# Sixteen float32 attention items with the softmax divided after the product

## The chip, the core and the metric

The kernel runs on one core of a Trainium2 chip. The metric is the device time of the whole program in microseconds (us). PE is TensorE (matrix products), PEld its weight loads, DVE is VectorE, ACT is ScalarE, POOL is GpSimd, SP issues the DMAs.

## What is computed

Windowed attention with a linear position bias, and two MLPs behind it, all in float32:

```python
B, H, S, D = 4, 8, 576, 64;  window = 128
scores = q @ k.T / sqrt(D)                       # per batch b and head h
scores = where(0 <= i - j < window, scores - slope[h] * (i - j), -1e9)
attn = exp(scores - max(scores, -1))
attn = attn / (sum(attn, -1) + 1e-9)
x = (attn @ v), heads side by side               # 2304 tokens x 512
h1 = x @ w_in;   x2 = (max(h1, 0) + alpha * min(h1, 0)) @ w_out     # d_ff = 2048
h2 = x2 @ w_in2; out = (h2 * sigmoid(1.702 * h2)) @ w_out2
```

## The kernel before

The attention is cut into 64 items (batch, part, head). Part 0 is the first 256 queries of a batch, in two chunks of 128: the first sees 128 keys, the second 256. Items 0 to 15 (part 0 of batches 0 and 1, `FP = 2 * H`) are computed with plain float32 products; from item 16 on operands are split into a high and a low half. Only items 0 to 15 are touched by the change. For such an item n the steps are:

- `a_qk` (L342): scores s in PSUM, two products with a 64-row operand.
- `a_bias` (L362, DVE): adds the bias, writes the negated scores to tt in SBUF and their row minimum to st.
- `a_exp` (L378, ACT): exponential of each chunk with the row extreme taken off, and the row sums into st.
- `a_recip` (L386, L387) and `a_norm` (L398), DVE: reciprocal of the sums, and each chunk times its reciprocal.
- `a_trans` (L411): three transposes of 128 x 128 through TensorE into pt in PSUM; `a_pt_hi` (L418, ACT) copies them to SBUF.
- `a_av` (L432): product with v as the stationary operand and pt as the moving one, one of 256 columns and one of 128; a float32 product is two passes, so four matrix records. vz is v of one head in its half of 128 columns, with zeros in the other half, so that an even and an odd head add up in one bank x.
- `a_x3` (L479 ACT, L107 DVE): x of a pair of heads is split into xh and xl, the input of the first MLP, feature-major.

Beside this, weights are decoded: they come as pairs of words through SP's DMA queue into four buffers ws; ACT scales (L147, L150), DVE shifts and adds (L154, L159), ACT casts the high half wh (L102) and DVE subtracts for the low half wl (L107). Layer 1 has 32 such chunks, two for each of 16 hidden slices.

The first loop (items 0 to 9) is the prologue; the second runs the MLP of a block of 256 tokens, one step f for a hidden slice: `m1_h` (L493) makes h from xh and xl, ACT and DVE make g and its halves gh and gl (L508, L518, L522, L107), and `m1_o` (L544) adds the product with the second weights, two steps later. Every second step carries one more attention item. Block 0 needs the x of items 0 to 7, that is four pairs; in block 0 the weight chunks are still being decoded. "gl 13" is the low half of g in step f = 13 of block 0.

The program is written in that order, but a scheduler sets the order within each engine; weight decoding is kept in program order among itself. Engines work in order. PSUM has eight banks: two for h, two for the output sums (pool ps_o, tags o0 and o1), four shared by the attention (pool ps_a).

## Time and profile before

| | |
|---|---|
| median of 3 runs | 948.61 us (948.21 to 950.05) |
| the profiled execution | 951.22 us, of it span 949.4 us |
| busy in the span | PE 98%, PEld 91%, DVE 72%, ACT 55%, POOL 9% |
| chain that ended last | PE 91%, DVE 2%, issue 1% |
| granted TensorE clock, mean | 0.999 |

How to read it: busy time counts an engine from the start to the end of each instruction, so instructions that overlap or wait inside (matrix products above all) look longer than they are. Where an engine is the limit, the time from one start to the next (the pitch) says what an instruction costs. The chain follows the last instruction back through whatever released it; what lies off it can still hold a buffer or a queue.

### The profile page before, as it was taken

Reading aid. Unit: us, or ns where it says so; the run is one execution under the profiler, and the core shown is the slowest. Engines: PE = TensorE matmul, PEld = TensorE weight load, DVE = VectorE, ACT = ScalarE, POOL = GpSimd, SP = SyncE. Lnnn points to the kernel's source line nnn. Section 1 sums busy time; section 2 is a strip of 40 time slices with the busy share of each in tenths; the row PEclk is TensorE's granted clock in tenths of the full one; section 3 lists DMA queues with packets and bytes.
Section 4 is the critical chain, followed back from the end, with each engine's and each line's share of the span. In section 5 each row is a group of like instructions: output and inputs, shape, how many; then the busy total and the mean of one; then the engine's idle time right before and its main releaser. Section 6 shows DMA issues by size and latency. Waiting matters only on the chain.

```text
span 949.4 us, 17872 instructions
## 1 busy us (share of the span) xinstructions
PE 926.7 (98%) x6536; PEld 862.2 (91%) x6536; DVE 687.6 (72%) x1743; ACT 526.7 (55%) x1325; POOL 89.7 (9%) x127
## 2 busy tenths in 40 slices
PE   6899999999999999999999999999999999999997
PEld 3698899999999999999988888888898899999997
DVE  6898876778888888888457753685333798878876
ACT  5999866667667676676344443564232553433333
POOL 1100211122222222222000000000000000000000
PEclk9999999999999999999999999999999999999999
DMA  9666511223222222221023344665332333433323
GB/s 242 205 217 209 183 54 55 66 68 91 69 67 91 67 68 91 67 90 44 1 89 110 112 128 169 203 227 199 117 124 99 134 134 117 151 133 132 132 72 112
DMA packets 44041, 112.45 MB, mean 118 GB/s; under 512 B 5041, under 2 KB 15153, under 8 KB 43953
## 3 DMA queue, kind: packets, MB, share of 16 engines
q1 hardware_dynamic: 43952, 111.31, 36.1%
q8 instruction: 51, 0.84, 0.4%
q14 instruction: 38, 0.30, 0.1%
HBM read 82.98 MB, written 28.31 MB: 117 GB/s over the span
## 4 chain that ended last, share of the span: by engine, by line
PE 91%; DVE 2%; issue 1%; ACT 0%; DVEq 0%; ACTq 0%
PE h L493 21%; PE h L591 21%; PE p L658 18%; PE o L544 17%; PE p L544 5%; PE x L444 3%; PE pt L411 3%; PE s L351 1%; PE s L352 1%; PE s L342 1%; DVE wl L107 0%; DVE wd L159 0%; ACT oh L102 0%; PE x L432 0%; DVE wd L154 0%
## 5 line engine op out<-in xcount | busy, mean ns | idle before, releaser
L493 PE MATMUL h<-xh,wh 128*128 128x256 f32 (+1 forms) x512 | 151.9, 298 | 1.4 <-ACT xh L479 1.4
L493 PE MATMUL h<-xh,wl 128*128 128x256 f32 (+1 forms) x512 | 152.3, 298 | 0.0
L493 PE MATMUL h<-xl,wh 128*128 128x256 f32 (+1 forms) x512 | 151.4, 296 | 0.0
L658 PE MATMUL p<-wh,oh 128*128 128x256 f32 x504 | 136.3, 284 | 1.0 <-ACT oh L102 0.6
L658 PE MATMUL p<-wl,oh 128*128 128x256 f32 x504 | 136.2, 283 | 0.0
L544 PE MATMUL o<-gh,wl 128*128 128x256 f32 x448 | 127.5, 286 | 0.0
L544 PE MATMUL o<-gh,wh 128*128 128x256 f32 x448 | 125.9, 286 | 0.7 <-ACT gh L522 0.7
L544 PE MATMUL o<-gl,wh 128*128 128x256 f32 x448 | 125.5, 281 | 1.1 <-DVE gl L107 1.1
L658 PE MATMUL p<-wh,ol 128*128 128x256 f32 x504 | 119.2, 283 | 0.4 <-DVE ol L107 0.4
L591 PE MATMUL h<-x2h,wh 128*128 128x512 f32 (+1 forms) x320 | 117.9, 368 | 0.0
L591 PE MATMUL h<-x2l,wh 128*128 128x512 f32 (+1 forms) x320 | 117.8, 368 | 0.0
L591 PE MATMUL h<-x2h,wl 128*128 128x512 f32 (+1 forms) x320 | 117.7, 368 | 0.0
L605 DVE TENSOR_TENSOR g<-h,sg 128x512 f32<-128x512 f32 (+1 forms) x80 | 51.0, 638 | 90.7 <-ACT sg L601 90.5
L601 ACT ACTIVATE sg<-h 128x512 f32<-128x512 f32 (+1 forms) x80 | 44.4, 555 | 108.5 <-PE h L591 108.3
L493 PEld LDWEIGHTS h<-xh,wh 128*128 128x128 f32 x512 | 96.3, 189 | 5.2 <-ACT xh L479 1.9
L493 PEld LDWEIGHTS h<-xh,wl 128*128 128x128 f32 x512 | 96.6, 189 | 3.9 <-DVE wl L107 0.6
L493 PEld LDWEIGHTS h<-xl,wh 128*128 128x128 f32 x512 | 97.0, 189 | 3.0 <-issue 0.3
L658 PEld LDWEIGHTS p<-wh,oh 128*128 128x128 f32 x504 | 96.5, 192 | 2.1 <-ACT oh L102 2.0
L658 PEld LDWEIGHTS p<-wl,oh 128*128 128x128 f32 x504 | 96.7, 192 | 0.1
L518 DVE SCALAR_TENSOR_TENSOR g<-n,beta,h 128x256 f32<-128x256 f32 x112 | 53.2, 475 | 54.1 <-ACT n L508 53.8
L508 ACT ACTIVATE n<-h 128x256 f32<-128x256 f32 x112 | 42.8, 383 | 87.8 <-PE h L493 87.3
L658 PEld LDWEIGHTS p<-wh,ol 128*128 128x128 f32 x504 | 86.5, 192 | 0.7 <-DVE ol L107 0.6
(105 smaller groups left out, 2203.0 us busy)
## 6 DMA issues: line engine op xcount, KB each, us to landing
ws<-in_w_in_dram SPq DMA_DIRECT2D x32, 512.0 KB, 3.9
ws<-in_w_out_dram SPq DMA_DIRECT2D x32, 512.0 KB, 3.7
raw<-in_u_dram SPq DMA_DIRECT2D x32, 512.0 KB, 3.5
g2d<-g SPq DMA_DIRECT2D x32, 512.0 KB, 3.1
gr<-g2d SPq DMA_DIRECT2D x32, 512.0 KB, 3.2
raw<-in_u_dram SPq DMA_DIRECT2D x16, 320.0 KB, 2.8
wd<-x2d SPq DMA_DIRECT2D x36, 128.0 KB, 2.9
out_dram<-ob SPq DMA_DIRECT2D x16, 256.0 KB, 3.4
```

The costliest lines, as they stand in the source:

```text
L342: nc.tensor.matmul(o[:, :keys], raw[:, c0 : c0 + rows], raw[:, 256 + kk : 256 + kk + keys], start=True, stop=True)
L351: nc.tensor.matmul(o[:, :n_], q, kh[:, ks : ks + n_], start=True, stop=False)
L411: nc.tensor.transpose(banks[bank][:, dst : dst + P], src, ident)
L444: nc.tensor.matmul(x[:, oc : oc + nq], v, p[:, col : col + nq], start=(i == 0 and k == 0), stop=(i == len(js) - 1 and k == 1), skip_group_ ...
L493: nc.tensor.matmul(ph, w[:, 0, c * P : (c + 1) * P], x[:, c, r : r + n], start=(c == 0 and i == 0), stop=(c == NC - 1 and i == 2),)
L508: nc.scalar.activation(n, ph, AF.Relu, scale=-1.0)
L518: nc.vector.scalar_tensor_tensor(g, n, beta[:, f : f + 1], ph, op0=ALU.mult, op1=ALU.add)
L544: nc.tensor.matmul(o, w[:, 1, c * P : (c + 1) * P], g, start=(f == 0 and (k == KM or c % 2 == 0) and i == 0), stop=(f == NF - 1 and i == 2 ...
L591: nc.tensor.matmul(ph[:, :n], w[:, f % 2, c * P : (c + 1) * P], x[:, c, :n], start=(c == 0 and i == 0), stop=(c == NC - 1 and i == 2),)
L601: nc.scalar.activation(sg[:, :n], ph[:, :n], AF.Sigmoid, scale=1.702)
L605: nc.vector.tensor_tensor(g[:, f % 2, :n], ph[:, :n], sg[:, :n], op=ALU.mult)
L658: nc.tensor.matmul(o[:, m, :], g[:, a, m * P : (m + 1) * P], w, start=(p == 0 and m == 0 and i == 0), stop=(p == NF // 2 - 1 and i == 2), ...
```

## The change

For items 0 to 15 the division moves behind the product. `f_sub` takes the row extreme off the negated scores in SBUF (first chunk on DVE, second on ACT). `a_trans` transposes these scores instead of the weights of the softmax, and `f_exp` takes the exponential while reading the transposes from PSUM and writes pt. `f_av` turns the product: pt is the stationary operand, and the moving one is v with a column of ones behind it, 65 columns, so that column 64 of the result is the sum. Per item there are three such products, into a bank xq that an even and an odd head share. `f_div` (every odd item, DVE) adds 1e-9 to the four columns of sums, takes the reciprocal and multiplies, into xq in SBUF, with queries on the partitions. `a_x3` first transposes xq back with two transposes into a bank x. `a_exp`, `a_recip`, `a_norm` and `a_pt_hi` do nothing for these items. For items below 8 the two banks are those of the output sums, idle until the first `m1_o`; for items 8 to 15 they come from the four shared ones. In the loops `f_exp` stands first in an item's turn, and `a_x3` comes one item earlier than before.

```diff
@@ -261,7 +261,8 @@
-    vzs = [apf.tile([P, 2, P], F32, name=f"vz{i}") for i in range(2)]
+    vzs = [apf.tile([P, 2, D + 1], F32, name=f"vz{i}") for i in range(2)]
+    xq = apf.tile([P, 2, 2, D], F32, name="xq")
@@ -324,8 +325,7 @@
         if n < FP:
-            d0 = (h % 2) * D
-            nc.gpsimd.tensor_copy(vzs[n % 2][:, :, d0 : d0 + D], vr)
+            nc.gpsimd.tensor_copy(vzs[n % 2][:, :, :D], vr)
             return
@@ -371,8 +371,28 @@
+    @stage
+    def f_sub(n, b, u, h, U):
+        if n >= FP:
+            return
+        tt, s = tts[n % 2], sts[n % 2]
+        for i, (c0, rows, kk, keys) in enumerate(U["chunks"]):
+            t = tt[:rows, i * 256 : i * 256 + keys]
+            if i:
+                nc.scalar.activation(t, t, AF.Identity, bias=s[:rows, i : i + 1], scale=-1.0)
+            else:
+                nc.vector.tensor_scalar(t, t, s[:rows, i : i + 1], -1.0, op0=ALU.subtract, op1=ALU.mult)
+
+    @stage
+    def f_exp(n, b, u, h, U):
+        if n < FP:
+            x, c, w = st["t", n][0]
+            nc.scalar.activation(pts[n % 2], x[:, :w], AF.Exp)
...
@@ -423,16 +447,37 @@
+    def early(tag, n, name):
+        pool, tag = (pso, tag) if n < H else (ps_a, "a")
+        return pool.tile([P, 2, T1], F32, tag=tag, name=name)
+
+    @stage
+    def f_av(n, b, u, h, U):
+        if n >= FP:
+            return
+        if h % 2 == 0:
+            st["xq", n // 2] = early("o0", n, "xq").rearrange("p c (h t) -> p c h t", h=2)
+        x = st["xq", n // 2]
+        pt, vz = pts[n % 2], vzs[n % 2]
+        for c, j, col in ((0, 0, 0), (1, 0, 128), (1, 1, 256)):
+            nc.tensor.matmul(
+                x[:, c, h % 2, : D + 1], pt[:, col : col + P], vz[:, j, :],
+                start=(c == j == h % 2 == 0), stop=(c == j), skip_group_check=True,
+            )
+
+    @stage
+    def f_div(n, b, u, h, U):
+        if n >= FP or h % 2 == 0:
+            return
+        s, x = sts[n % 2], st["xq", n // 2]
+        r, f = (s[:, i : i + 4].rearrange("p (c h) -> p c h", c=2) for i in (8, 12))
+        nc.vector.tensor_scalar(r, x[:, :, :, D], 1e-9, None, op0=ALU.add)
+        nc.vector.reciprocal(f, r)
+        nc.vector.tensor_tensor(xq, x[:, :, :, :D], f.unsqueeze(3).to_broadcast([P, 2, 2, D]), op=ALU.mult)
...
     def a_av(n, b, u, h, U):
         if n < FP:
-            x = st["x", n] = st["x", n - 1] if h % 2 else ps_a.tile([P, 512], F32, tag="a", name="x")
-            pt, vz = pts[n % 2], vzs[n % 2]
-            for j in range(2):
-                nc.tensor.matmul(
-                    x[:, j * P : 256], vz[:, j, :], pt[:, j * 256 : 256 + j * P],
-                    start=(h % 2 == 0 and j == 0), stop=(h % 2 == 1 and j == 1), skip_group_check=True,
-                )
             return
@@ -470,7 +515,9 @@
         if n < FP:
-            xp = st["x", n]
+            xp = early("o1", n, "x").rearrange("p c t -> p (c t)")
+            for i in range(2):
+                nc.tensor.transpose(xp[:, i * P : (i + 1) * P], xq[:, i, :, :], ident)
...
@@ -744,7 +791,7 @@
-        a_av(n - 2)
+        f_exp(n - 1)
         a_split_v(n)
@@ -753,21 +800,19 @@
         a_bias(n)
+        f_sub(n)
         w("split")
-        a_exp(n)
-        a_recip(n - 1)
+        f_av(n - 1)
         w("shift")
-        a_norm(n - 1, "dve")
-        a_trans(n - 1)
         w("add")
         w_ahead()
+        f_div(n - 1)
+        a_trans(n, True)
         w("scale")
-        a_x3(n - 2)
         if n % 4 == 0:
             w("split")
             w("shift")
-        a_pt_hi(n - 1, 0)
-        a_pt_hi(n - 1, 1)
+        a_x3(n - 1)
...
@@ -806,13 +844,16 @@
         m1_h(k, f)
         if s % 2 == 0:
+            f_av(m)
             a_trans(m)
...
             a_pt_hi(m, 1)
+            f_div(m)
             a_bias(n)
+            f_sub(n)
             wd("shift")
@@ -823,6 +864,10 @@
             a_av(m)
+            a_trans(n, True)
+            f_exp(n)
+            if m < FP:
+                a_x3(m)
```

What this makes of the order, at three places; names are as above, a number behind a name is a buffer, and ISA stands for L362 (bias) and L159 (the decoding add). First DVE at the fourth xl, the last that block 0 needs. Before:

```order
L362 ISA tt_147,st_149<-s,relht 128x256
L362 ISA st_149 128x1
L154 TENSOR_SCALAR wd<-wd 128x512
L159 ISA wd<-ws,wd 128x1024 x2
L386 TENSOR_SCALAR st_149<-st_149 128x2
L387 RECIPROCAL st_149<-st_149 128x2
L398 TENSOR_SCALAR tt_147<-tt_147,st_149 128x128
L398 TENSOR_SCALAR tt_147<-tt_147,st_149 128x256
L107 TENSOR_TENSOR xl<-x,xh 128x256
L107 TENSOR_TENSOR wl_498<-wd,wh_497 128x512
```

And now:

```order
L159 ISA wd<-ws,wd 128x1024
L383 TENSOR_SCALAR tt_146<-tt_146,st_148 128x128
L107 TENSOR_TENSOR xl<-x,xh 128x256
L474 TENSOR_SCALAR st_149<-xq 128x4
L475 RECIPROCAL st_149<-st_149 128x4
L107 TENSOR_TENSOR wl_465<-wd,wh_464 128x512
L154 TENSOR_SCALAR wd<-wd 128x512
L476 TENSOR_TENSOR xq<-xq,st_149 128x256
L159 ISA wd<-ws,wd 128x1024
```

The same xl now follows 9 decoding adds from the start of the program instead of 12, and the norms around it have become one subtraction (L383) and the three rows of a division (L474 to L476), the first of which comes right behind it.

Then TensorE shortly before the first dense products of block 0, where two items end their way and two more are on it. Before:

```order
L411 MATMUL pt<-ident,tt_146 128x128 x3
L432 MATMUL x<-pt_161,vz_159 128x256
L432 MATMUL x<-pt_161,vz_159 128x128
L432 MATMUL x<-pt_160,vz_158 128x256
L432 MATMUL x<-pt_160,vz_158 128x128
L411 MATMUL pt<-ident,tt_147 128x128
L342 MATMUL s<-raw_144 128x128
L342 MATMUL s<-raw_144 128x256
L411 MATMUL pt<-ident,tt_147 128x128 x2
L493 MATMUL h<-xh,wh_223 128x256
L493 MATMUL h<-xh,wh_286 128x256
```

And now:

```order
L520 MATMUL x<-ident,xq 128x128 x2
L463 MATMUL xq<-vz_159,pt_162 128x65 x3
L540 MATMUL h<-xh,wh_231 128x256
L540 MATMUL h<-xh,wh_296 128x256
L435 MATMUL pt<-ident,tt_146 128x128 x3
L540 MATMUL h<-xl,wh_231 128x256
L540 MATMUL h<-xh,wl_232 128x256
L540 MATMUL h<-xl,wh_296 128x256
L540 MATMUL h<-xh,wl_297 128x256
L520 MATMUL x<-ident,xq 128x128 x2
```

The products of 256 and 128 columns are gone; there are three of 65 columns with pt as weights, and the pair is transposed back (L520) before the h products that read it.

Last, DVE just ahead of gl 13, the last row of each. Before:

```order
L518 SCALAR_TENSOR_TENSOR g<-n,beta,h 128x256
L107 TENSOR_TENSOR xl<-x,xh 128x256
L107 TENSOR_TENSOR wl_1123<-wd,wh_1122 128x512
L362 ISA tt_147,st_149<-s,relt 128x128
L362 ISA st_149 128x1
L362 ISA tt_147,st_149<-s,relt 128x256
L362 ISA st_149 128x1
L107 TENSOR_TENSOR wl_1123<-wd,wh_1122 128x512
L107 TENSOR_TENSOR wl_1229<-wd,wh_1228 128x512
L107 TENSOR_TENSOR gl<-g,gh 128x256
```

And now:

```order
L107 TENSOR_TENSOR wl_1060<-wd,wh_1059 128x512
L154 TENSOR_SCALAR wd<-wd 128x512
L408 TENSOR_SCALAR st_149<-st_149 128x2
L159 ISA wd<-ws,wd 128x1024
L565 SCALAR_TENSOR_TENSOR g<-n,beta,h 128x256
L409 RECIPROCAL st_149<-st_149 128x2
L154 TENSOR_SCALAR wd<-wd 128x512
L420 TENSOR_SCALAR tt_147<-tt_147,st_149 128x128
L420 TENSOR_SCALAR tt_147<-tt_147,st_149 128x256
L159 ISA wd<-ws,wd 128x1024
L107 TENSOR_TENSOR wl_1125<-wd,wh_1124 128x512 x2
L107 TENSOR_TENSOR gl<-g,gh 128x256
```

Where the bias of a later item stood right before gl 13, there is now already the reciprocal and norm of an item further on (L408 to L420, an item of the second kind).

## Rows read from the trace of the kernel before

**Rows 1.** Stretch, busy us (count) of PE, PEld, DVE, ACT, POOL; clock, DMA share, GB/s.

```profile
5.45:47.00 41.55, 32.35 (x119) 22.63 (x120) 33.83 (x120) 33.33 (x88) 5.14 (x11) 1.00 0.83 230
47.00:78.00 31.00, 31.00 (x231) 28.09 (x232) 27.51 (x80) 27.35 (x70) 1.75 (x5) 1.00 0.64 206
78.00:106.00 28.00, 25.43 (x184) 22.43 (x184) 27.16 (x77) 26.86 (x70) 3.47 (x7) 1.00 0.74 234
```

**Rows 2.** Chain that ended last, in order of time: start, us, what.

```profile
69.29 0.65 PE x L432 x4
...
82.29 0.37 PE pt L411 x2
...
87.56 1.18 PE o L544 x10
...
90.39 0.60 DVE wl L107
...
101.02 0.50 DVE tt L398
```

**Rows 3.** DVE in order of time: start, us, engine, line, operation, tiles, shapes, [idle before].

```profile
5.45 0.29 DVE L362 CUSTOM_DVE_ANT_0 tt<-s,relht 128x128 f32<-128x128 f32 x1 [5.45 <-PE s L342]
...
6.01 0.08 DVE L362 DVE_READ_ACCUMULATOR2_ANT st<- 128x1 f32 x1
...
39.63 0.28 DVE L398 TENSOR_SCALAR tt<-tt,st 128x128 f32<-128x128 f32 x1
39.82 0.42 DVE L154 TENSOR_SCALAR wd<-wd 128x512 int32<-128x512 int32 x1
40.16 0.35 DVE L398 TENSOR_SCALAR tt<-tt,st 128x256 f32<-128x256 f32 x1
40.42 0.42 DVE L107 TENSOR_TENSOR xl<-x,xh 128x256 fp32r<-128x256 f32 x1
40.75 0.69 DVE L159 CUSTOM_DVE_ANT_0 wd<-ws,wd 128x1024 uint16<-128x1024 uint16 x1
41.37 0.15 DVE L386 TENSOR_SCALAR st<-st 128x2 f32<-128x2 f32 x1
...
46.85 0.42 DVE L107 TENSOR_TENSOR xl<-x,xh 128x256 fp32r<-128x256 f32 x1
...
104.99 0.41 DVE L107 TENSOR_TENSOR gl<-g,gh 128x256 fp32r<-128x256 f32 x1
```

**Rows 4.** ACT in order of time, same columns.

```profile
38.97 0.48 ACT L418 COPY pt<-pt 128x384 f32<-128x384 f32 x1
39.34 0.41 ACT L378 ACTIVATE tt<-tt,st 128x128 f32<-128x128 f32 x1
...
40.24 0.67 ACT L147 ACTIVATE wd<-ws 128x512 f32<-128x512 f32 x1
```

**Rows 5.** Weight loads beside products of 64 columns, in order of time.

```profile
234.24 0.19 PEld L444 LDWEIGHTS x<-ptl,vp 128*128 128x128 f32 x1
234.35 0.19 PEld L544 LDWEIGHTS o<-gh,wl 128*128 128x128 f32 x1
```

**Rows 6.** What DVE waited for, 0 to 47 us: us in total, times, longest.

```profile
DVE tt L362 <- PE pt L411: 3.3, 3, 1.7
DVE st L386 <- ACT tt L378: 1.1, 3, 0.7
DVE wd L154 <- ACT wd L147: 0.7, 3, 0.3
DVE wl L107 <- ACT wh L102: 0.5, 1, 0.5
```

**Rows 7.** The same from 47 to 106 us.

```profile
DVE wd L154 <- ACT wd L147: 0.7, 2, 0.4
DVE st L386 <- ACT tt L378: 0.6, 1, 0.6
```

**Rows 8.** What TensorE waited for, 0 to 46 us, same columns.

```profile
PE x L432 <- ACT pt L418: 3.1, 3, 1.7
```

More of the change, by code (lines that the diff above doesn't have):

```diff
@@ L373, in a_exp @@
     @stage
+    def f_sub(n, b, u, h, U):
[14 more added lines that the diff above has]
+    @stage
     def a_exp(n, b, u, h, U):
         tt, s = tts[n % 2], sts[n % 2]
+        if n < FP:
+            return
         for i, (c0, rows, kk, keys) in enumerate(U["chunks"]):
@@ L385, in a_recip @@
         m = len(U["chunks"])
+        if n < FP:
+            return
         nc.vector.tensor_scalar(s[:, 8 : 8 + m], s[:, 4 : 4 + m], 1e-9, None, op0=ALU.add)
@@ L391, in a_norm @@
         tt, s = tts[n % 2], sts[n % 2]
-        for i, (c0, rows, kk, keys) in enumerate(U["chunks"]):
+        for i, (c0, rows, kk, keys) in enumerate(U["chunks"] if n >= FP else ()):
             t = tt[:rows, i * 256 : i * 256 + keys]
@@ L400, in a_trans @@
     @stage
-    def a_trans(n, b, u, h, U):
+    def a_trans(n, b, u, h, U, fp=False):
         tt = tts[n % 2]
+        if (n < FP) != fp:
+            return
         banks = [ps_a.tile([P, 512], F32, tag="a", name="pt") for _ in range(1 + u)]
@@ L415, in a_pt_hi @@
     def a_pt_hi(n, b, u, h, U, i):
-        if i <= u:
+        if i <= u and n >= FP:
             x, c, w = st["t", n][i]
-            nc.scalar.copy(pts[n % 2] if n < FP else ar["pth"][:, c : c + w], x[:, :w])
+            nc.scalar.copy(ar["pth"][:, c : c + w], x[:, :w])
     @stage
@@ L424, in a_pt_lo @@
             sub("dve", ar["ptl"][:, c : c + w], x[:, :w], ar["pth"][:, c : c + w])
+    def early(tag, n, name):
[4 more added lines that the diff above has]
+        if n >= FP:
+            return
+        if h % 2 == 0:
[10 more added lines that the diff above has]
+        if n >= FP or h % 2 == 0:
+            return
+        s, x = sts[n % 2], st["xq", n // 2]
[3 more added lines that the diff above has]
+        nc.vector.tensor_tensor(xq, x[:, :, :, :D], f.unsqueeze(3).to_broadcast([P, 2, 2, D]), op=ALU.mult)
     @stage
@@ L707, in tile_window_attention__then__two_mlps @@
     for t in vzs:
-        nc.gpsimd.memset(t, 0.0)
+        nc.gpsimd.memset(t, 1.0)
     for t in sts:
@@ L778, in tile_window_attention__then__two_mlps @@
     a_split(n)
-    for i in range(2):
-        a_pt_lo(n - 2, i)
-    a_recip(n - 1)
-    a_norm(n - 1, "dve")
-    a_av(n - 2)
-    a_x1(n - 2)
-    a_x2(n - 2)
-    a_x3(n - 2)
+    f_exp(n - 1)
     at0.close()
@@ L839, in tile_window_attention__then__two_mlps @@
             m1_lo(k, f, "dve")
-            a_x3(n - 1)
+            if m >= FP:
+                a_x3(m)
         if k == 0:
```

## The prediction

> **What bounds the kernel now.** The page first: by its first lines TensorE is busy for nearly the whole span, so at first sight an edit on other engines can't pay. The edit touches only the sixteen float32 items, so the stretch to read is the one in which they run, the first 110 us; from the table by stretches [rows 1] the reader should take that VectorE (DVE) is busy 33.8 of the 41.6 us to 47 us, 27.5 of the next 31, and 27.2 of the last 28, with ScalarE (ACT) just as full. TensorE is not: up to 47 us it has 119 products in 41.55 us, against 231 in the next 31. Its busy time there is mostly latency. Then the chain of waits [rows 2]: TensorE's products carry it through the sixties to the eighties, and from 90 to 101.5 us it lies on DVE, in weight decoding (wd, wl) and norms, before TensorE takes it over for good. So there are three regimes: a prologue held by DVE, ACT and the loads, a stretch held by TensorE, and a stretch where DVE is late again because 32 weight chunks must be decoded beside the attention.
>
> The end of that third regime is a single instruction: DVE's gl of step 13 of the first block (start 104.99 us [rows 3]). Behind it TensorE has no wait of note. From about 137 us on both programs have the same order of work on TensorE, so what the change does is decided before that. I therefore write the time as start-up + DVE work before gl 13 + DVE idle before it + TensorE work left after it.
>
> **How I count.** In the order of each program I counted every instruction ahead of a point and multiplied by its pitch, the time from its start to the next one's start. On DVE [rows 3]: norm 0.20 (128 columns) and 0.26 (256), shift 0.34, decoding add and wl 0.60 [rows 2, 3], xl from PSUM 0.33, the two small ones of the reciprocal 0.17 each (their durations), the bias of both chunks 0.56. On ACT [rows 4]: the two exponentials with their sums 0.90, the copy of pt 0.37. On TensorE [rows 2]: 0.118 for a product of 256 columns, so 895.3 us of work in the whole program before and 897.1 after, of which 75.2 and 79.2 stand ahead of the first use of gl 13. Check on before: 5.45 of start-up, 85.8 of DVE work, 12.05 idle (7.72 + 3.49 + 0.84 [rows 1]) make 103.3 against 104.99 seen.
>
> **The change, part by part.** *DVE, per float32 item:* two norms (0.46) and the reciprocal pair (0.34) go, 0.80 x 16 = 12.8. The subtraction of the first chunk comes in, 128 columns like a norm, 0.20 x 16 = 3.2. Per pair of items come an add and a reciprocal on four columns, 0.20 and 0.17, and one product of 256 columns out of PSUM, priced like xl at 0.335: 0.705 x 8 = 5.6. Net -4.0 us. But the new order also pulls work of later items ahead of gl 13: two more biases, three ptl, three q, three more items normalised, two xp, one xl, less one wl, +6.6 us. So DVE has 88.5 instead of 85.8 to do before gl 13: **+2.65**.
>
> *ACT, per item:* 0.90 + 0.37 go; the subtraction of the 256-column chunk and one exponential over 384 columns of PSUM come in, each between the pitch of the copy, 0.37, and its duration, 0.48 [rows 4]. About 0.5 us per item is saved, 8 us in all. ACT's work ahead of the fourth xh falls from 32.3 to 22.9 us, partly because 10 chunks are scaled before it and not 13. ACT is never later than DVE in my counts, so this pays only through the waits of the others.
>
> *TensorE, per item:* the product was four passes of 0.65 us together [rows 2, 5]. It becomes six passes of 65 columns, each with its own weight load. The nearest row is a pair of 64-column products: their weight loads start 0.11 us apart [rows 5], so a pass costs 0.11, not the 0.055 that 65 columns would take at the old passes' rate (768 columns in 0.65 us). 6 x 0.11 = 0.66, no gain. If the loads were as badly hidden as in transposes with other shapes beside them (0.37 for two [rows 2]), a pass would be 0.19, 0.5 us more per item. I take 0.11, whose row has the same 128 x 128 weights. Two transposes a pair are added, 0.11 to 0.19 each [rows 2, 5]: +1.8 us at the lower price. All of it lies ahead of gl 13, where by my counts TensorE is early: its dense work starts near 40.4 us (below) with 24.6 us done, 79.2 stand before its use of gl 13, so it is there at 95.0, while DVE needs 5.45 + 88.5 + 9.45 = 103.4. These 8.4 us hide the 1.8; without the cover it would cost that, or 11 at the dear prices (16 x 0.5 + 16 x 0.19), and then some 3 would show. The new order also has TensorE do 2.2 us of later items before gl 13: **-2.2** on what is left after it.
>
> *Memory:* GpSimd's copies of v stay, at another place. In PSUM the pair's product now holds a bank from the even item to the division; for the first eight items that is the idle bank of the output sum, for the last eight one of the four shared ones. I price that at nothing while the pair moves on within two steps.
>
> *DVE idle:* this is the term I can't count. Up to 47 us DVE waited 3.3 us for TensorE's transposes and 1.1, 0.7 and 0.5 us for ACT [rows 6], 5.6 together, and TensorE in turn waited 3.1 us for ACT's pt [rows 8]. With ACT 9 us lighter I let half of the 5.6 go, -2.8. It can't all go: the DMA engines are 83% busy there [rows 1], and a chunk must land before it is decoded. Of the 3.5 us in the TensorE-held stretch I let 0.8 go, of the 1.3 us that the two largest waits for ACT make there [rows 7]. Against that, DVE now waits at each of the eight divisions for TensorE's product, which waits for ACT's exponential. The nearest row is the wait for the old exponential's sum (1.1 us for the ten items up to 47 us [rows 6], about 0.1 each); I take +1.0 for eight. Net **-2.6**, with bounds -6.4 (nearly all waits for ACT and transposes go, none come) and +2.5 (none go, each division waits 0.3).
>
> Sum: +2.65 - 2.2 - 2.6 = **-2.15 us**. The profiled execution has 951.22 us, 949.4 of it span; it becomes 949.1. On the median of 948.61 us that is 946.5.
>
> What the reader should notice is what is not in the sum. The fourth xl, with which TensorE's dense work begins, stands behind 26.5 us of DVE work and not 32.9, so dense matmuls should begin near 40 us (5.45 + 26.5, some 7 of idle as now, and a step to TensorE) and no longer at 47. That gain is mostly given back, since only 9 chunks are decoded by then and not 12, and TensorE waits for DVE later.
>
> **The rivals.** (a) *The idle time stays:* DVE's waits up to 47 us follow the loads, not ACT. For it: 83% of DMA time. Against: the waits that the profile names there are for ACT and TensorE, but for the first scores. Then only +2.65 - 2.2 is left: 949.1.
> (b) *The division turns into a wait, slower:* DVE works in order, so at each division everything behind it, weight decoding above all, waits for exponential, product and their hand-overs. If each costs the mean wait for a transpose (3.3 us in 3 waits, 1.1 [rows 6]), eight make 8.8: 0.45 - 3.6 + 8.8 = +5.7, 954.3. It turns slower than the bound below from 0.6 us a division. For it: three dependent engines. Against: in the order, decoding mostly stands between product and division.
> (c) *ACT frees more than I let it:* idle falls by 6.4: 948.61 + 0.45 - 6.4 = 942.7. For it: TensorE's own longest waits before 46 us, but for the first loads, are for ACT's pt [rows 8].
> (d) *The clock falls in the prologue.* The granted clock is 1.00, the 2.4 GHz level, in every stretch [rows 1], also while TensorE is thinly used. At the 1.2 GHz level its 24.6 us of work before the fourth xl would take twice that, TensorE would hold the prologue, and its dense work would start near 54 us (5 + 49): 54 + 897.1 - 24.6 = 926.5 against 103.3 + 820.1 = 923.4 before, some 3 us slower, 951.7. The Trainium skill, page "TensorE: Matmul & The Clock Gate", section "Part 4: PE-mode transpose", says that the full clock doesn't engage for transpose-mode work; by that rule replacing product columns by transposes would bring this case about. The trace of before, with transposes in the same thin stretch at full clock, speaks against it.
>
> **How the numbers follow.** A measurement of this kernel tells about 0.2% (1.9 us) from no change. My forecast's own range is 942 to 948. Forecast and (c) together, as far as they pass the bound, get 0.47; (a) and the part of the forecast within the bound 0.33; (b) 0.17 and (d) 0.03, slower. The range goes from 942, just past (c), to 951.5, the upper bound of the idle term (0.45 + 2.5 = +2.95); most of (b) is left out above.
>
> **What would show it.** Right: the fourth xl near 40 us (47 before); DVE idle between 5.45 us and gl 13 near 9.5 us; gl 13 near 105 us, hardly moved; TensorE waiting for gl, gh or norms between 80 and 105 us by several us more than before; 0.66 us per turned product. Wrong: waits of DVE for xq above 0.6 us each (b), a granted clock below 1.00 before 50 us (d), idle unchanged (a), or TensorE saturated right through to 110 us, which would say that DVE was not the bound and that the whole early start is kept, some 7 us.

## Result and the profile after

The changed kernel takes 960.56 us (median of 4 runs, 956.95 to 967.1), the kernel before 949.33 us beside it: 1.0117 times as long, interval 1.0078 to 1.0156. It is about 11 us slower; 946.5 us was forecast, with 951.5 us as the upper end.

The profiled execution after has 967.1 us, 965.3 of it span, and is the slowest of the four; before it was 951.22 and 949.4. The first section of the page and its row of the granted clock (40 slices of 24 us) read:

```profile
PE 943.1 (98%) x6584; PEld 880.0 (91%) x6584; DVE 683.9 (71%) x1719; ACT 521.5 (54%) x1277; POOL 90.8 (9%) x127
...
PEclk9999799999999999999999999999999999999999
```

The shares are as before, within a point; the one new thing is a clock of 0.7 in the fifth slice. The stretches of [rows 1], after the change (columns as there):

```profile
5.45:47.00 41.55, 38.82 (x143) 29.79 (x143) 25.98 (x92) 26.19 (x50) 4.90 (x12) 1.00 0.73 204
47.00:78.00 31.00, 31.00 (x216) 28.51 (x216) 25.13 (x71) 23.35 (x52) 1.49 (x4) 1.00 0.56 178
78.00:106.00 28.00, 23.27 (x160) 21.95 (x160) 24.45 (x71) 24.18 (x58) 5.00 (x8) 0.88 0.64 206
```

DVE, on whose work and idle time the sum of the prediction rests, is less busy in all three: 25.98 us for 33.83, 25.13 for 27.51, 24.45 for 27.16. It is less busy because it waits. What it waited for up to 47 us (in all, times, longest), which answers to [rows 6]:

```profile
DVE tt L362 <- PE s L342: 11.2, 7, 5.2
DVE wd L154 <- ACT wd L147: 2.3, 1, 2.3
DVE st L474 <- PE xq L463: 2.0, 3, 1.1
DVE wl L107 <- ACT wh L102: 2.0, 2, 1.9
DVE xl L107 <- ACT xh L526: 1.3, 1, 1.3
```

The wait of 5.2 us is the one for the first scores, which both kernels have. The other 6.0 us for scores are six waits, and the wait for the new product (xq) is another 2.0. In the kernel before the waits for scores in the same stretch are two, of which one, 1.2 us, is not the first:

```profile
DVE tt L362 <- PE s L342: 6.6, 2, 5.4
```

From 47 to 106 us after the change, in place of [rows 7]:

```profile
DVE wl L107 <- ACT wh L102: 4.1, 4, 1.4
DVE tt L362 <- PE s L342: 3.6, 2, 2.2
DVE st L474 <- PE xq L463: 0.5, 2, 0.3
```

And TensorE, which before had no wait of note there, waits from 47 to 122 us for the weights:

```profile
PE h L540 <- ACT wh L102: 6.1, 4, 2.5
```

The two marks of [rows 3], the fourth xl (46.85 us before) and gl 13 (104.99 us), are now at:

```profile
50.07 0.42 DVE L107 TENSOR_TENSOR xl<-x,xh 128x256 fp32r<-128x256 f32 x1 [0.54 <-ACT xh L526]
...
122.80 0.42 DVE L107 TENSOR_TENSOR gl<-g,gh 128x256 fp32r<-128x256 f32 x1
```

The sum of the prediction, with the profiled times put in. "DVE work" is the time from DVE's first instruction to gl 13 less its idle time there, "rest" is from gl 13 to the end of the span:

| us | before | forecast change | after | change |
|---|---|---|---|---|
| first DVE instruction | 5.4 | 0 | 5.2 | -0.2 |
| DVE work before gl 13 | 87.5 | +2.65 | 91.2 | +3.7 |
| DVE idle before gl 13 | 12.0 | -2.6 | 26.4 | +14.3 |
| rest | 844.4 | -2.2 | 842.5 | -1.9 |
| span | 949.4 | -2.15 | 965.3 | +15.9 |

Three terms are near where they were forecast, the idle time is not, and it makes the result of this execution. The agreement of the rest is partly luck: kernels that differ little from this one have 839 to 847 us there (table below). The experiments look for what made the idle time.

One reading of before has to be corrected first. The page and the tables by stretches print a clock of 1.00 also where the trace has no record of the clock. The records of the kernel before begin at 32.5 us, with a rise to full; those of the kernel after begin at 54.2 us, and show three falls to half (1.2 GHz) at 88.3, 98.6 and 112.2 us, 13.7 us together. That the time ahead of the rise is at half rate is seen in the products: the four records of a score product (L342) take 1.65 us ahead of it and 0.92 after it. So TensorE's busy time up to 47 us, which the prediction calls mostly latency, was in part work at half rate. Shortly before and after the rise of the kernel before:

```profile
28.26 1.65 PE L342 MATMUL s<-rawf 64*128 64x128 f32 x4
...
32.92 0.92 PE L342 MATMUL s<-rawf 64*128 64x128 f32 x4
```

So the first theory was the clock (C): the thin product of 65 columns leaves TensorE at half rate for 22 us more.

### The profile page after: what moved, and what is told of

It is laid out like the page before. It is cut to its first block, busy times and chain, and to the rows that moved or that the text cites. A ratio compares the mean times of both kernels' runs of the same rounds, so it can differ in the third digit from the quotient of the medians.

```text
span 965.3 us, 17877 instructions
## 1 busy us (share of the span) xinstructions
PE 943.1 (98%) x6584; PEld 880.0 (91%) x6584; DVE 683.9 (71%) x1719; ACT 521.5 (54%) x1277; POOL 90.8 (9%) x127
## 5 line engine op out<-in xcount | busy, mean ns | idle before, releaser
L540 PE MATMUL h<-xh,wl 128*128 128x256 f32 (+1 forms) x512 | 154.5, 302 | 0.8 <-DVE wl L107 0.7
L540 PE MATMUL h<-xl,wh 128*128 128x256 f32 (+1 forms) x512 | 153.4, 300 | 0.0
L591 PE MATMUL o<-gl,wh 128*128 128x256 f32 x448 | 126.3, 283 | 0.0
L540 PEld LDWEIGHTS h<-xh,wl 128*128 128x128 f32 x512 | 98.6, 193 | 4.4 <-DVE wl L107 1.4
L705 PEld LDWEIGHTS p<-wh,oh 128*128 128x128 f32 x504 | 96.4, 192 | 2.5 <-ACT oh L102 2.4
L565 DVE SCALAR_TENSOR_TENSOR g<-n,beta,h 128x256 f32<-128x256 f32 x112 | 53.1, 475 | 59.7 <-ACT n L555 59.5
```

The source lines that it names most:

```text
L540: nc.tensor.matmul(ph, w[:, 0, c * P : (c + 1) * P], x[:, c, r : r + n], start=(c == 0 and i == 0), stop=(c == NC - 1 and i == 2),)
L565: nc.vector.scalar_tensor_tensor(g, n, beta[:, f : f + 1], ph, op0=ALU.mult, op1=ALU.add)
L591: nc.tensor.matmul(o, w[:, 1, c * P : (c + 1) * P], g, start=(f == 0 and (k == KM or c % 2 == 0) and i == 0), stop=(f == NF - 1 and i == 2 ...
L705: nc.tensor.matmul(o[:, m, :], g[:, a, m * P : (m + 1) * P], w, start=(p == 0 and m == 0 and i == 0), stop=(p == NF // 2 - 1 and i == 2), ...
```

## Experiments

All medians and intervals are against runs of the kernel before on the same chip. The table holds what the traces say; the text refers to it. "Old" and "new" places are explained at experiment 9. "Falls" is the time at half rate after the rise, without the last 3 to 6 us of the span, which are at half rate in every trace; 12th and 32nd are the ends of the split (wl) of these weight chunks. Clock, work and chunks belong to the one profiled execution of each.

| kernel | median us | ratio | rise | falls | DVE work | DVE idle | rest | 12th | 32nd |
|---|---|---|---|---|---|---|---|---|---|
| before | 949.3 | 1 | 32.5 | 0 | 87.5 | 12.0 | 844.4 | 52.8 | 109.8 |
| after (new places) | 960.6 | 1.0117 | 54.2 | 13.7 | 91.2 | 26.4 | 842.5 | 64.2 | 129.8 |
| e2, before, extra products | 950.6 | 1.0023 | 16.1 | 3.4 | 85.1 | 15.0 | 847.8 | 51.3 | 106.5 |
| e3, new places, old product | 958.4 | 1.0086 | 24.4 | 10.2 | 91.6 | 18.7 | 840.9 | 55.0 | 122.6 |
| e4, new places, 128 columns | 961.4 | 1.0114 | 25.4 | 6.8 | 96.4 | 17.4 | 839.4 | 59.5 | 122.0 |
| e5, after, items held | 959.3 | 1.0122 | 32.0 | 13.7 | 84.9 | 20.7 | 845.9 | 56.9 | 115.2 |
| e6, e4, items held | 963.7 | 1.0156 | 25.5 | 20.5 | 85.6 | 25.0 | 845.7 | 59.5 | 120.7 |
| e7, e3, items held | 955.3 | 1.0053 | 26.7 | 6.8 | 80.3 | 22.3 | 846.2 | 56.1 | 115.0 |
| e8, after, all items held | 966.2 | 1.0171 | 60.7 | 6.8 | 85.0 | 28.4 | 846.9 | 64.6 | 126.3 |
| e10, after, more decoding | 963.1 | 1.0147 | 32.6 | 3.4 | 93.0 | 15.8 | 843.4 | 54.2 | 123.2 |
| e13, old places | 947.8 | 0.9987 | 35.6 | 6.8 | 84.1 | 12.4 | 845.0 | 49.1 | 108.9 |
| e14, old places, 128 columns | 948.9 | 0.9998 | 29.6 | 6.8 | 82.3 | 12.7 | 846.2 | 50.1 | 103.0 |
| e15, old operations, new places | 961.5 | 1.0145 | 26.0 | 6.8 | 93.8 | 14.2 | 844.9 | 57.7 | 118.7 |
| e16, old places, more decoding | 950.0 | 1.0008 | 53.3 | 0 | 83.0 | 11.6 | 848.4 | 46.0 | 101.1 |
| e17, old places in the prologue | 954.6 | 1.0065 | 34.8 | 6.8 | 87.8 | 13.8 | 843.7 | 48.8 | 111.3 |
| e19, e16 with 128 columns | 950.5 | 1.0001 | 27.3 | 6.8 | 83.5 | 11.5 | 845.6 | 48.3 | 102.2 |

**1 and 2: extra products, to raise the clock early.** A tile `dm` of ones, and into both kernels (the last lines as in the one before; the changed one has `f_sub` there too):

```diff
+    def warm(m):
+        for _ in range(m):
+            x = ps_h.tile([P, DM], F32, tag="h", name="h")
+            nc.tensor.matmul(x, dm[:, :P], dm, start=True, stop=True)
+    warm(8)
     a_load(0, (0,))
...
+        warm(2)
         a_bias(n)
         w("split")
+        warm(2)
```

> The changed kernel with extra matrix products that nothing reads (a constant tile of ones, 512 columns, BF16, into the idle PSUM banks of the first layer): 8 ahead of the first scores and 4 in each step of the prologue; all else is as it was. Theory C (the clock of TensorE is what the change lost: it rises at 54.2 us in place of 32.5 us, and the matrix work at half rate bounds the prologue): the rise comes well ahead of 32 us, the fourth xl ends between 38 and 44 us (50.07 in the changed kernel), and the time is 942 to 952 us. Rival O (the order of the work is worse, weights are decoded later whatever the clock): the extra products change nothing of that order, the time stays at 955 to 965 us. Rival D (the division is a wait of VectorE for TensorE and back): 955 to 965 us too, with VectorE's wait for xq as long as before (2.4 us between 20 and 60 us).

> The kernel before with the same extra products at the same places. Theory C: the rise comes ahead of 32.5 us here too. In the kernel before VectorE and ScalarE were busy for 3.1 of each 4 us up to 60 us, so the prologue gains only the part in which they waited for scores at half rate: 944 to 949 us. If TensorE at half rate bounds nothing there: 948 to 951 us, with the rise early all the same.

e1: 963.48 us, 1.0132 (1.0111 to 1.0152), as slow as without. Its profiled execution lay 12 us above this median, and the clock rose late in it (49.7 us), so it doesn't tell whether an early rise would help: inconclusive. e2: the rise came at 16.1 us, and the kernel took 950.58 us, 1.0023 (1.0008 to 1.0037), 0.2% slower. The 48 products are 0.216 us apart at full clock where they follow one another, 10.4 us of TensorE's time, more at half rate, so what an early rise may have saved, they may have spent; but a large gain there was not. (Its first DVE instruction is the fill of the tile, at 0.9 us, so its idle time in the table counts some 4.4 us more than that of the others.)

**3: the new subtraction and exponential, with the old product.** The division and the transposes back are left out.

```diff
-        for c, j, col in ((0, 0, 0), (1, 0, 128), (1, 1, 256)):
+        for j in range(2):
             nc.tensor.matmul(
-                x[:, c, h % 2, : D + 1], pt[:, col : col + P], vz[:, j, :],
+                x[:, j * P : 256], vz[:, j, :], pt[:, j * 256 : 256 + j * P],
...
```

> One part of the change alone: the maximum subtracted, scores transposed, exponential read from PSUM, all as in the changed kernel; but the product with v is the one of the kernel before (v with zeros at rest, 256 and 128 columns of exponentials streamed). The division by the sums, the two transposes back and their waits are left out, so the attention output is not divided. Theory C, with the thin turned product as its cause: the clock rises near 32 us (28 to 36), it does not fall again between 84 and 122 us, and the time is 941 to 950 us. If the rise comes late all the same (45 us or later), the cause in the clock is another part, and the time is 950 us or more. Rival O: 955 to 962 us, for the scores, the subtraction and the weights are issued as in the changed kernel. Rival D: 941 to 950 us with a rise that may lie anywhere.

958.37 us, 1.0086 (1.0071 to 1.0101). The rise came early, as theory C wants, but the time hardly fell: C and D (the division) both miss. The first product with the second weights of block 0 began 9.4 us earlier than before (43.2 for 52.6 us), and all of it was lost again by the 32nd chunk, 122.6 us for 109.8.

**4: the turned product with 128 columns.**

```diff
-    vzs = [apf.tile([P, 2, D + 1], F32, name=f"vz{i}") for i in range(2)]
+    vzs = [apf.tile([P, 2, P], F32, name=f"vz{i}") for i in range(2)]
...
-                x[:, c, h % 2, : D + 1], pt[:, col : col + P], vz[:, j, :],
+                x[:, c, h % 2, :], pt[:, col : col + P], vz[:, j, :],
```

> The changed kernel with one size changed: the turned product streams 128 columns (v, the ones, and 63 further columns that are not read) in place of 65. Nothing else moves. Theory C in the form 'too few columns a pass': the clock rises earlier than 54 us (30 to 45 us) although there is more to stream, and the time falls to 946 to 957 us. Theory C in the form 'too much transposing, whatever the product': the rise stays at 50 us or later and the time is 957 to 968 us. Rivals O and D: 957 to 966 us, the rise anywhere.

961.44 us, 1.0114 (1.0085 to 1.0143). The rise did come at 25.4 us; score products around it:

```profile
19.60 1.65 PE L342 MATMUL s<-raw 64*128 64x128 f32 x4
25.00 1.12 PE L342 MATMUL s<-rawf 64*128 64x128 f32 x4
27.28 0.92 PE L342 MATMUL s<-rawf 64*128 64x128 f32 x4
```

It won nothing. Theory C falls as the cause of the whole 11 us: a rise 7 us sooner than in the kernel before stands beside the full loss. With the fall at 42.5 us TensorE was at half rate for 32.3 us in all, as long as in the kernel before (32.5). One thing in the expectation doesn't hold, that nothing else moves: the scheduler's order on DVE differs from that of the changed kernel from 17 us on, so the two rises don't tell what the columns alone do.

**5 to 8: items held back.** In e3, e4 and the changed kernel, 21 to 22 items had had their bias on DVE when the 32nd chunk was split; in the kernel before, 18. New theory (R): attention runs ahead of the weights and takes DVE from them. The edit pins the bias behind what stands before it on DVE, for items 16 to 23 (in e8 for items 3 to 23):

```diff
-            nc.vector.tensor_tensor_reduce(
+            ins = nc.vector.tensor_tensor_reduce(
...
+            if i == 0 and 16 <= n < 24:
+                tc.keep_in_program_order(ins)
```

> The changed kernel with one issue order added: on VectorE the masked-scores reduction of items 16 to 23 may no longer be issued ahead of the work that stands before it in the program. Nothing else is added or left out. In the changed kernel 21 items have had this reduction when the 32nd weight chunk has been split (129.8 us), in the kernel before 18 (109.8 us). Theory R (attention runs ahead of the weights: items 18 to 20, which block 0 does not need yet, take some 9 to 10 us of VectorE that the weight chunks of block 0 wait for): the 32nd chunk is split at 117 to 122 us, TensorE's waits of block 0 shrink by 8 to 10 us, and the time is 948 to 954 us. Theory C (what is lost is the clock, which falls three times between 84 and 122 us and rises late): the rise stays late, and so the time stays at 955 to 965 us.

> The same issue order added to the kernel whose turned product streams 128 columns, in which the granted clock rose at 25.4 us and was full from 49.3 us, and which took 961 us all the same. Theory R: the 32nd chunk is split at 110 to 114 us in place of 122.0 us, and the time is 945 to 953 us. Theory C: no change, 957 to 963 us. If the two causes add (late clock and items ahead), this one is faster than the hold alone by 3 us or more.

> The same issue order added to the kernel with the new subtraction and exponential and the old product (no division and no transposes back, so the attention output is not divided). It began block 0 9.4 us earlier than the kernel before (43.2 against 52.6 us) and still took 958 us. Theory R: the 32nd chunk is split at 110 to 114 us in place of 122.6 us, and the time is 942 to 950 us. Theory C: 955 to 959 us, since its clock had been full from 24.5 to 79 us already.

> The changed kernel with the same issue order for items 3 to 23, so that the items do not run ahead of the weights in the prologue either: 8 items at the 8th chunk, as in the kernel before, in place of 10. Theory R in the form 'every item ahead costs its VectorE time': below the hold from item 16 by 1 to 3 us, 945 to 952 us. If the prologue is bound by TensorE at half rate (theory C for that part alone), holding items there brings nothing or costs: 950 to 958 us, with a rise at 50 us or later.

959.27, 963.65, 955.28 and 966.21 us; only e7 gained, 3 us. 18 items were now ahead of the 32nd chunk, and DVE had 6 to 11 us less work before gl 13 (e3 to e7: 91.6 to 80.3), but its idle time grew by 3.6 and 7.6 us where the clock rose at nearly the same time (e3 to e7, e4 to e6; e6 also has more falls). In e5 idle time fell, 26.4 to 20.7 us, beside a rise 22 us sooner, and the median did not follow. So I read the items ahead as filling idle time rather than making it: R falls.

The pair of e5 and the changed kernel shows more. Up to 87 us (in e5) the order of work is the same on TensorE, DVE, ACT and GpSimd; the held items come later. The two traces keep step up to 32 us, the changed kernel 0.4 us ahead. Then the clock rises in e5 and not in the changed kernel, and by 55 us the latter is 7.4 us behind and stays so up to 78 us. Score products of the changed kernel and of e5 shortly behind the rise of e5, and the fourth xl of e5 (50.07 us in the changed kernel):

```profile
37.39 1.65 PE L342 MATMUL s<-raw 64*128 64x128 f32 x4
...
35.21 0.92 PE L342 MATMUL s<-raw 64*128 64x128 f32 x4
...
43.55 0.42 DVE L107 TENSOR_TENSOR xl<-x,xh 128x256 fp32r<-128x256 f32 x1
```

So at the new places a late rise cost an execution some 7 to 8 us, by this one pair, and one order of work rose at 54.2 us in one execution and at 32.0 in another. The clock is a second cause of the profiled time of the changed kernel, though not of the loss that is there without it: this execution of e5 still took 958.47 us.

In e7 the handing over of the chunks between the two engines shows, DVE's and ACT's waits of 47 to 106 us:

```profile
DVE wl L107 <- ACT wh L102: 5.8, 6, 1.5
```

```profile
ACT wd L147 <- DVE wl L107: 4.8, 7, 1.0
```

Each engine waits for the other, with DVE busy 22.22 of the 28 us from 78 to 106 us. Time was lost to waits between engines that had too little to do; that turned the question to what stands how near to what.

**9: the new operations at the old places.** In the kernel before, item n had its bias in step n, norms and transposes in step n+1, product in step n+2. The change moved subtraction and transposes into step n, and the exponential, product, division and transposes back into step n+1: each step stands one item nearer to the one it needs ("new places"). Here the same operations go where their forerunners stood ("old places"); the prologue part of the edit, block 0 likewise:

```diff
-        f_exp(n - 1)
+        f_av(n - 2)
         a_split_v(n)
...
-        f_sub(n)
         w("split")
-        f_av(n - 1)
+        f_sub(n)
+        f_div(n - 2)
         w("shift")
+        a_trans(n - 1, True)
         w("add")
         w_ahead()
-        f_div(n - 1)
-        a_trans(n, True)
         w("scale")
+        a_x3(n - 2)
...
-        a_x3(n - 1)
+        f_exp(n - 1)
```

> All the new operations of the changed kernel, put at the places that their forerunners had in the kernel before: transposes and exponential of item n-1 (the changed kernel: of item n, in the same step as its subtraction), turned product, division and transposes back of item n-2 (n-1). Same work, one item more between each step and the next. Theory P (the places are what the change lost: steps that need each other stand closer, so VectorE and ScalarE wait for one another in their queues, and the weight chunks behind them are late): the 32nd weight chunk is split at 105 to 113 us (129.8 in the changed kernel, 109.8 before), and the time is 943 to 952 us. Theory N (the new operations themselves): 955 to 963 us. Theory C (the clock, for the thin product is still there): the rise comes at 45 us or later, and 953 to 963 us.

> The same with the turned product streaming 128 columns in place of 65, which gave a rise at 25 us at the new places. Theory P: 943 to 952 us, within 3 us of the 65 columns at the old places. Theory C as a second cause: the rise comes by 35 us, and the time is 3 us or more below that of the 65 columns. Theory N: 955 to 963 us.

947.82 us, 0.9987 (0.9970 to 1.0003), and 948.85 us, 0.9998 (0.9983 to 1.0014). The whole loss is gone, with every new operation kept. gl 13 of e13 is ahead of the kernel before:

```profile
101.81 0.42 DVE L107 TENSOR_TENSOR gl<-g,gh 128x256 fp32r<-128x256 f32 x1
```

DVE's waits up to 47 us, beside those of after above:

```profile
DVE tt L362 <- PE s L342: 5.5, 2, 5.3
DVE tt L362 <- PE pt L435: 2.5, 3, 1.6
DVE wd L154 <- ACT wd L147: 2.4, 2, 2.3
DVE st L474 <- PE xq L463: 0.7, 1, 0.7
```

But for the first scores, the wait for scores is down from 6.0 to 0.2 us, that for the new product from 2.0 to 0.7. N (the operations) falls, and so does C as a second cause at the old places: with 128 columns, and the rise 6 us sooner, the time is the same.

**10: more decoding in the prologue of the changed kernel.** `if n % 4 == 0:` becomes `if n % 2 == 0:`, twice.

> The changed kernel, all at its own places, with two more weight chunks decoded in the prologue (the extra round of decoding stands in every second step in place of every fourth), and so two fewer left to block 0. Theory P, in the form 'the decoding of block 0 starts too far behind': the 32nd chunk is split some 5 us earlier, and the time is 950 to 957 us. If the prologue has no room for them (the chunks have not landed, or TensorE at half rate bounds the step): 957 to 964 us, no change.

963.08 us, 1.0147 (1.0122 to 1.0173), no help. In the profiled execution the 12th and 32nd chunks did come sooner than after the change, 54.2 and 123.2 us for 64.2 and 129.8. But its rise is early (32.6 us), and with the rise of e5 they come at 56.9 and 115.2 without the added rounds, so what the rounds themselves bring is not told apart.

**11: the converse, old operations at the new places.**

Part of the edit; block 0 likewise:

```diff
...
         a_bias(n)
+        a_exp(n)
         w("split")
-        a_exp(n)
-        a_recip(n - 1)
+        a_av(n - 1)
         w("shift")
-        a_norm(n - 1, "dve")
-        a_trans(n - 1)
         w("add")
         w_ahead()
+        a_recip(n)
+        a_norm(n, "dve")
+        a_trans(n)
...
```

> The converse: all the old operations of the kernel before (exponential ahead of the transposes, sums, reciprocal, scaling, old product), put at the places of the changed kernel: each step of an item follows the step it needs one item sooner. Theory P (the places are what the change lost): slower than the kernel before by 5 to 14 us, 954 to 963 us, with VectorE waiting for TensorE's scores and ScalarE for the transposes between 20 and 52 us for 8 us or more each (3.0 and 3.1 us in the kernel before). If the places hurt only together with the new operations: 947 to 952 us.

961.51 us, 1.0145 (1.0094 to 1.0195): as slow as the changed kernel, with none of its new operations. That the places are the cause is shown from both sides. The clock doesn't make this loss: TensorE was at half rate for 32.8 us in all (rise and falls), in the kernel before for 32.5. The waits were not those expected: between 20 and 52 us DVE waited 1.3 us for scores and ACT 3.3 for the transposes, not 8 or more each. Up to 47 us:

```profile
DVE tt L362 <- PE s L342: 8.5, 6, 5.3
DVE st L386 <- ACT tt L378: 4.5, 6, 1.5
```

The sum of the exponential, needed in the same step, is now what DVE waits for most behind the first scores (4.5 us, 1.1 in [rows 6]). Here most of the delay of gl 13 (113.2 us) is work of later items that DVE did meanwhile (93.8 for 87.5 us), and only some 2 us are idle time.

**12 and 13: the two halves.** e17 has the old places in the prologue and the new ones in block 0, e18 the reverse.

> The changed kernel with the old places in the prologue alone (items 0 to 9); in block 0 all stands where the changed kernel has it. VectorE's waits of 20 to 52 us were 12.5 us in the changed kernel and 2.9 us with all at the old places, those of 52 to 112 us 6.9 and 7.1 us. Theory P in the form 'it is the prologue': 946 to 952 us. In the form 'it is block 0': 955 to 962 us. Both in part: between.

> The other half: the new places in the prologue, the old places in block 0 (items 10 to 15). Theory P in the form 'it is the prologue': 955 to 962 us, with the clock rising at 45 us or later. In the form 'it is block 0': 946 to 952 us.

954.62 us, 1.0065 (1.0040 to 1.0090), and 953.16 us, 1.0054 (1.0024 to 1.0084). Each half gives back about half: 5.9 and 7.4 us of the 12.7 between 960.56 and 947.82. In e17 the 12th chunk is as early as at the old places (48.8 us) and the 32nd late by 2.4 us against e13. The profiled execution of e18 lay 10 us above its median, so it is not in the table; its order is that of the changed kernel up to 51 us, and its rise came at 58.7 us, which fits the cost of a late rise seen beside e5.

**14 and 15: what bounds the kernel at the old places.** e16 is e13 with the decoding of e10; e19 also has the 128 columns.

> All new operations at the old places, and two more weight chunks decoded in the prologue (every second step in place of every fourth). With all at the old places the time was 947.8 us, and VectorE had 98.0 us of work in the first 120 us. If block 0 is now bound by the decoding of its last chunks: 943 to 947 us. If the prologue has no room for more: 948 to 953 us.

> All new operations at the old places, two more chunks decoded in the prologue, and the turned product streaming 128 columns. The kernel with the two more chunks had its 32nd chunk at 101.1 us and TensorE busy for all of 52 to 112 us, but a clock that rose only at 53.3 us; with 128 columns the rise came at 25 to 30 us in each of three kernels. If the clock before 53 us is now what bounds it: 942 to 946 us, faster than both kernels. If not: 947 to 951 us, as its two parents (948.9 and 950.0 us), and the clock of the prologue is worth nothing here at any place.

950.04 us, 1.0008 (0.9994 to 1.0021), and 950.46 us, 1.0001 (0.9990 to 1.0012). In e16 the 32nd chunk came 7.8 us sooner than in e13, and nothing followed. e16 is the best witness on the clock at the old places: its TensorE stayed at half rate as long as that of the changed kernel,

```profile
46.71 1.65 PE L342 MATMUL s<-raw 64*128 64x128 f32 x4
...
53.45 0.92 PE L342 MATMUL s<-raw 64*128 64x128 f32 x4
```

and it is as fast as the kernel before, since DVE decoded meanwhile, 33.39 of the first 41.55 us for 25.98 after the change:

```profile
5.45:47.00 41.55, 38.14 (x141) 29.97 (x142) 33.39 (x106) 33.39 (x64) 3.92 (x12) 1.00 0.90 255
47.00:78.00 31.00, 31.00 (x223) 28.72 (x223) 28.64 (x79) 25.97 (x58) 1.90 (x5) 1.00 0.69 211
78.00:106.00 28.00, 28.00 (x231) 27.01 (x231) 25.11 (x68) 22.45 (x53) 2.92 (x4) 1.00 0.61 193
```

No version is told apart from the kernel before on the fast side; e13 comes nearest (0.9987, interval up to 1.0003).

## Why the prediction was wrong

**What held.** The frame: gl 13 ends the stretch that decides. In the table the rest behind it is 839 to 848 us in all sixteen traces, while it moves itself from 100 to 123 us. The counts of work, within the scatter of the table: DVE's +2.65 was +3.7, TensorE's -2.2 was -1.9. And the price of the turned product: six records take 0.78 us from first start to last end at full clock, by pitch 0.11 us a pass, as read from the weight loads [rows 5]:

```profile
63.94 0.78 PE L463 MATMUL xq<-vz,pt 128*128 128x65 f32 x6
```

At half rate, where most of them ran, they took 1.38, 0.21 a pass. The net of the change per operation, put at 4.0 us less on DVE, shows over the whole span: DVE is busy 683.9 us after and 687.6 before, 3.7 less. At the old places (e13) the kernel is even then at most 0.3% faster (by the interval), which says that the freed work itself bought next to nothing.

**The step that failed** is the one that begins "With ACT 9 us lighter I let half of the 5.6 go". It took the idle time as a thing that shrinks with the load of the engine one waits for, and put it at -2.6. The runs show in its place that the time goes by the distance between dependent steps: 960.6 us with the new operations at the new places, 947.8 at the old ones. How the distance acts is read from the order and the waits. The kernel before left one item between norm, transposes and product; when TensorE was late, DVE had the next item's work and a weight chunk in front of it. The change took that item out. Now DVE's bias waited for scores (six waits, 6.0 us), ACT's exponential for the transposes (6.0 us in 5 waits from 20 to 52 us, for 3.1 in 4 before), DVE's division for the product, and the weight decoding stood behind them in both queues: 9 chunks were split at 51.8 us where 12 were at 52.8. ACT's waits, after the change and before:

```profile
ACT pt L389 <- PE pt L435: 6.0, 5, 2.0
...
ACT pt L418 <- PE pt L411: 3.1, 4, 1.2
```

The bounds of the term, -6.4 to +2.5, were both worked out from the old waits with the old distance, and the answer, +14.3 in the profiled execution, lay outside. Some 7.4 us of it is the late rise (the lag behind e5); the +7 left by these two numbers is an estimate, and still outside. In e4, e10 and e15, new places with an early rise, idle time before gl 13 is only some 5, 4 and 2 us above the kernel before, but 9, 6 and 6 us more work of DVE stands there, since it did later items meanwhile. So the price of the places shows partly as idle time and partly as work done too early. The order rows ahead of the prediction hint at it: the first row of a division right behind xl, with no decoding between.

**The early start** did not come: the fourth xl was at 50.07 us and not near 40, with 17.2 us of idle time ahead of it where 7 were allowed. With the early rise of e5 it was at 43.55, with 11.0 us.

**Rival (b)** had the right kind of mechanism, a wait in DVE's queue with the decoding behind it, at the wrong instruction. The waits for xq are 2.5 us in 5 up to 106 us (0.5 each, below its point of 0.6); those for scores, which the change doesn't touch, are larger.

**Rival (d)** describes what the trace after shows, a rise at 54.2 us, and was given 0.03 because I read 1.00 [rows 1] as a measured clock where there was no record; the kernel before was itself at half rate up to 32.5 us. Its price of some 3 us was too low at the new places, where the late rise cost 7 to 8 (the changed kernel beside e5). But the clock doesn't tell the places apart: TensorE was at half rate (rise and falls) for 32.8 us in e15 and 32.5 in the kernel before, with medians of 961.5 and 949.3 us, and for 42.4 and 53.3 us in e13 and e16, with 947.8 and 950.0. The rule that rival (d) names, that transposes don't engage the full clock (the Trainium skill, "TensorE: Matmul & The Clock Gate", "Part 4: PE-mode transpose"), is not tested by any run here: with 65 and with 128 columns the transposes are the same, and so is the whole order of work up to 87 us in the two executions that rose at 54.2 and 32.0 us. The three falls after the change stand beside waits of TensorE for wh (1.1, 1.9 and 2.5 us); in e4 there is one fall, at 42.5 us, and the same time. How much a fall adds where TensorE is waited for was not measured by itself.

**What stays open:** which of the moved steps costs most. The halves of the program are told apart, the steps of an item are not. Each edit also made the scheduler order the engines anew, so a kernel differs from its neighbour by more than the lines shown; the two sides of the old and new places agree all the same. Why the clock rises late in one execution and early in another is not known, nor how many of the executions without a trace had the late rise.

## What to carry to other kernels

When an edit makes a chain of steps shorter and moves its steps nearer together, price the two apart: first put the new operations at the old distances, then move them. In queues that are worked off in order, the item that lies between two dependent steps is what hides the other engine's delay, and whatever is pinned behind the waiting instruction (here the weights) pays for it. Look at the clock of the execution in the trace before its waits are taken for those of the kernel. Before a clock of 1.00 is taken from a table, check it by the duration of one repeated product.

## What the hardware showed that was not expected

The rise of the granted clock came anywhere from 24 to 61 us in kernels whose TensorE work differs little (16 us with extra products), and for one order of work at 54.2 us in one execution and at 32.0 in another. What a late rise costs goes by the order: 7 to 8 us at the new places, where DVE waited for scores (the changed kernel beside e5), and no loss that shows at the old ones, where DVE decoded meanwhile (e16, 53.3 us, 950.0 us). Passes of 128 columns cost no more than those of 65: at full clock both start 0.11 us apart, at half rate 0.21. Six of 128 columns in e4:

```profile
63.31 0.83 PE L463 MATMUL xq<-vz,pt 128*128 128x128 f32 x6
```

The times agree (961.4 for 960.6 us, 948.9 for 947.8). That fits the reading that passes of this size are held by their weight loads [rows 5].
